# Two more batches of a fused attention and Fourier-mixing kernel take the folded token transform, under a new table of priorities

## The chip, the cores and the metric

The kernel runs on one NeuronCore of one Trainium2 chip. The metric is device time in microseconds (us). Before the change three runs gave 577.18, 578.38 and 578.51 us; their median is 578.38. One further execution, the profiled one, took 576.98 us, and every duration quoted below is from it. Its instructions span 575.2 us; the remaining 1.8 us lie around them.

The names of the engines in the profile: PE is TensorE (matrix products), PEld its weight loads, DVE is VectorE, ACT is ScalarE, POOL is GpSimd, and SP issues transfers.

## The reference

For 8 batches, 12 heads, 448 tokens and head size 64, the kernel computes cosine attention, a real-valued Fourier mix over tokens and features, a normalisation and a two-layer network:

```python
q_n = q / (norm(q) + 1e-6);  k_n = k / (norm(k) + 1e-6)
attn = softmax(q_n @ k_n.T / tau)            # per head
x = (attn @ v), heads side by side           # (8, 448, 768)
X = fft(x, axis=tokens); X = fft(X, axis=features)
u = x + real(X)
un = (u - mean(u)) / sqrt(var(u) + 1e-6)
out = u + relu(un @ w_ch1) @ w_ch2           # 768 -> 3072 -> 768
```

## The kernel before

**Planner.** The program does not write its instruction order by hand. Each step is an `Op` with a name such as `qk00_4` (step, then batch), a duration from a table (`TIMES`), a priority and its dependencies. `Plan.schedule` (line 257) plays the program through in modelled time and takes, on every engine, the ready step with the lowest priority number among those that can start first. The result is a fixed order of instructions for each of the queues PE, ACT, DVE, POOL and SP, with semaphores between them. After all steps are made, line 729 adds a number from the table `SHIFT` to the priority of single steps by name and occurrence. So `SHIFT` moves steps within the order, and nothing else. A step that may run on ACT or DVE goes where the planner finds room.

**Work of one batch.** (1) `norm` or `first_norm`: load q and k, square them on ACT (line 883), sum them on DVE (885), scale them (on POOL from batch 2 on, line 896), transpose them. (2) `attn`: for each of 6 pairs of heads the scores `qk` on PE (line 973 for three key tiles, two heads each on half of the rows; line 986 for the tail of 64 keys), the exponential on ACT (951), the products with v on PE (1004, 1010), the division on DVE (1028, 1030). (3) `fold`: sums and differences of mirrored tokens (n and 448-n) and of mirrored features on DVE (1047, 1054, 1081, 1098). (4) `fsum`: the transform over tokens on PE (1138 or 1134), evacuated by ACT or DVE (1159, 1160). (5) `fft`: the transform over features on PE (1188, 1191), its halves joined on DVE (1222) and added to x, with the sum for the mean (1233). (6) normalisation on ACT and DVE (1270 to 1282), a transpose by DMA, and (7) `ffn`: the two-layer network on PE (1350, 1445, 1494), with its evacuations (1366, 1514, 1530) and sums (1593).

**Interleaving.** Products of the network have a priority number above 5000, so that they fill PE wherever the attention and transform of the next batch have nothing ready. The network of batch b therefore lies between the pieces of attention and transform of batch b+1.

**The token fold.** `TF` (line 26) is 4, and a batch b with b >= TF handles its tokens differently. The 449 query columns of a score product (225 for tokens 0 to 224, 224 and one more for the mirrored ones) are given in four slices of 128, 97, 128 and 97 columns instead of two of 225 (`parts`, lines 936 to 938), so that token n and token 224-n meet at the same partition. Then `fold` multiplies half of its result by a mask (`z`, line 1091), forms sums and differences of tokens n and 224-n (`hb`, line 1094), and `fsum` needs for every frequency one product where it had two to add up (line 1134 instead of 1138; 16 products of 113 columns in a batch instead of 16 of 225). The table of cosines for this is rewritten once, in place, after the last unfolded batch (`ct`, line 1146). Because token 224 stands elsewhere, `fft` adds one more row (line 1258, one partition of 768 elements), and the lists of row numbers for the scattered output are made separately (`IDX2`, lines 626 to 632). How the scores of a batch are grouped into steps does not depend on `TF`: batches 1 to 3 take two key tiles in a step, batches 4 to 7 take three (lines 958 to 963).

Of the kernel before, what the change touches and what calls it, by code (L numbers as in the profile page):

```python
# [25 lines left out]
TF = 4  # L26
# [54 lines left out]
    "iotad": {0: 76.7149}, "tpd": {1: 15.2941}, "ktd0": {0: 169.0303}, "ix3": {0: -59.6164}, "ix4": {0: 735.3976}, "vz1": {0: 116.8365},  # L81
    "pads": {0: 761.6515}, "sins": {0: 15.0098}, "ldt0": {0: 217.8585}, "ldt1": {0: -95.8889}, "sind": {0: -207.551}, "sinp": {0: 240.8715},
# [1715 lines left out]
```

## Time and profile before

| | |
|---|---|
| profiled execution | 576.98 us |
| its span | 575.2 us, 16313 instructions |
| PE busy | 555.8 us, 97% of the span |
| DVE busy | 430.6 us, 75% |
| ACT busy | 385.3 us, 67% |
| POOL busy | 220.3 us, 38% |
| DMA | 62.20 MB, mean 108 GB/s |

A share of the span is a mean over very different stages. A table by stage (the view of windows) says in which stage an engine is full, the view of waits says for whom PE waited, and the chain that ended last gives single steps in order of time with the time each of them took before the next one began.

### The profile page before, as it was taken

How to read it: one execution, taken by the hardware profiler on the slowest of the kernel's cores; microseconds unless marked ns; L12 is line 12 of the kernel's file. 1: busy time of each engine (PE TensorE's matmuls, PEld its weight loads, DVE VectorE, ACT ScalarE, POOL GpSimd, SP SyncE). 2: the span in 40 equal slices, each digit the busy share in tenths (PEclk: the TensorE clock that was granted, in tenths of full speed). 3: DMA queues.
4: the chain of work that ended last, by engine and by line, in shares of the span. 5: the costliest groups of instructions: out<-in, count | busy, mean ns of one | idle time of the engine just before them, and what ended most of it. 6: DMA issues, size and time to landing. Idle time of an engine off the chain costs nothing.

```text
span 575.2 us, 16313 instructions
## 1 busy us (share of the span) xinstructions
PE 555.8 (97%) x6766; PEld 436.2 (76%) x6766; DVE 430.6 (75%) x917; ACT 385.3 (67%) x724; POOL 220.3 (38%) x332
## 2 busy tenths in 40 slices
PE   3899999999999999999999999999999999989997
PEld 3569787676787686878788787778778787959694
DVE  8989968996669869975669669776778579986262
ACT  7898885564876885687558875577637853747270
POOL 7534414356329544612370724523270210041303
PEclk9999999999999999999999999999999999999999
DMA  9999999975459739952595429743591210023001
GB/s 188 224 233 171 166 186 130 171 152 111 111 94 103 178 76 135 142 127 62 112 121 93 102 80 147 150 84 85 89 113 29 43 57 28 2 43 72 28 28 56
DMA packets 187898, 62.20 MB, mean 108 GB/s; under 512 B 166800, under 2 KB 185616, under 8 KB 187824
## 3 DMA queue, kind: packets, MB, share of 16 engines
q1 hardware_dynamic: 129856, 38.35, 33.7%
q0 software_dynamic: 57968, 22.81, 30.9%
q8 instruction: 53, 0.87, 0.6%
q14 instruction: 21, 0.17, 0.1%
HBM read 51.90 MB, written 11.01 MB: 109 GB/s over the span
## 4 chain that ended last, share of the span: by engine, by line
PE 60%; DVE 4%; ACT 2%; issue 0%; DVEq 0%; ACTq 0%
PE PS L1494 23%; PE PS L1350 20%; PE PS L1445 6%; PE PS L1010 4%; PE PS L973 3%; DVE U L1233 1%; PE PS L1004 1%; PE PS L986 1%; ACT E L951 1%; DVE ACG L1222 1%; ACT F L1275 1%; PE PS L1134 1%; PE PS L1191 1%; DVE SM L885 1%; DVE HQ L1593 1%
## 5 line engine op out<-in xcount | busy, mean ns | idle before, releaser
L1350 PE MATMUL PS<-UNT,W1b 128*128 128x256 bf16 (+1 forms) x1872 | 186.1, 256 | 1.2 <-DMA UNT<-F 0.6
L1350 PEld LDWEIGHTS PS<-UNT,W1b 128*128 128x128 bf16 x1872 | 155.5, 98 | 20.1 <-issue 2.7
L951 ACT ACTIVATE E<-PS 128x900 bf16<-128x900 f32 (+1 forms) x192 | 148.0, 827 | 19.1 <-PE PS L973 16.6
L1494 PE MATMUL PS<-W2b,HQ 128*128 128x384 bf16 x768 | 133.1, 326 | 0.0
L896 POOL TENSOR_TENSOR QH<-STG,SM 128x256 bf16<-128x256 f32 x126 | 82.3, 679 | 91.9 <-DVE SM L702 73.3
L1494 PEld LDWEIGHTS PS<-W2b,HQ 128*128 128x128 bf16 x768 | 73.3, 98 | 46.2 <-issue 0.7
L1519 POOL TENSOR_TENSOR OUTB<-OUTB,U 128x192 f32<-128x192 f32 x66 | 43.2, 675 | 138.5 <-ACT OUTB L1514 137.3
L1366 ACT ACTIVATE HQ<-PS 128x512 bf16<-128x512 f32 x81 | 48.2, 595 | 40.0 <-PE PS L1350 39.5
L1494 PE MATMUL PS<-TX,HQ 128*128 128x384 bf16 (+2 forms) x408 | 69.7, 321 | 1.8 <-ACT MV L1278 1.6
L883 ACT ACTIVATE QH<-STG 128x384 f32<-128x384 f32 x84 | 42.7, 520 | 25.8 <-DVE SM L885 21.3
L1494 PEld LDWEIGHTS PS<-TX,HQ 128*128 128x128 bf16 x408 | 38.4, 98 | 25.7 <-ACT MV L1278 2.0
L1593 DVE TENSOR_TENSOR HQ<-HQ 128x1536 bf16<-128x1536 bf16 (+1 forms) x69 | 49.5, 721 | 9.9 <-ACT HQ L1366 7.1
L885 DVE TENSOR_REDUCE SM<-QH 128x6 f32<-128x384 f32 x84 | 44.7, 544 | 11.3 <-ACT QH L883 11.0
L1010 PE MATMUL PS<-VB,E 128*128 128x65 bf16 x1152 | 51.4, 193 | 0.0
L1366 DVE TENSOR_SCALAR HQ<-PS 128x512 bf16<-128x512 f32 x45 | 31.0, 688 | 23.8 <-PE PS L1350 23.4
L1010 PEld LDWEIGHTS PS<-VB,E 128*128 128x128 bf16 x1152 | 47.7, 97 | 1.2
L1552 POOL DMA_INDIRECT out_dram<-OUTB,IDX x21 | 23.8, 1134 | 56.9 <-DVE OUTB L1530 51.7
L1004 PE MATMUL PS<-VZ,E 128*128 128x130 bf16 x192 | 41.6, 219 | 0.5 <-ACT E L951 0.2
L973 PE MATMUL PS<-QK 64*128 64x225 bf16 (+2 forms) x864 | 39.6, 227 | 0.1
L1233 DVE SCALAR_TENSOR_TENSOR U<-ACG,X 128x768 bf16<-128x768 f32 (+4 forms) x39 | 39.1, 1015 | 0.8
L1530 DVE TENSOR_TENSOR OUTB<-PS,OUTB 128x384 f32<-128x384 f32 x33 | 18.2, 553 | 25.7 <-PE PS L1494 21.9
L1514 ACT ACTIVATE OUTB<-PS 128x384 f32<-128x384 f32 x33 | 16.1, 488 | 29.5 <-PE PS L1494 29.1
(191 smaller groups left out, 793.6 us busy)
## 6 DMA issues: line engine op xcount, KB each, us to landing
STG<-in_q_dram SPq DMA_DIRECT2D x18, 384.0 KB, 4.0
STG<-in_k_dram SPq DMA_DIRECT2D x18, 384.0 KB, 3.8
VB<-in_v_dram POOLq DMA_DIRECT2D x24, 192.0 KB, 7.1
W1b<-in_moe_w_ch_dram POOLq DMA_DIRECT2D x12, 384.0 KB, 7.7
W2b<-in_moe_w_ch_dram POOLq DMA_DIRECT2D x12, 384.0 KB, 7.2
out_dram<-OUTB SPq DMA_DIRECT2D x7, 384.0 KB, 3.4
W2b<-in_q_dram SPq DMA_DIRECT2D x2, 576.0 KB, 10.0
W2b<-in_k_dram SPq DMA_DIRECT2D x2, 576.0 KB, 10.7
```

What stands on the lines that cost most here:

```text
L885: P.add("dve", lambda v, o=SS[:, i, H // ns * x:H // ns * (x + 1)], sq=sq: v.tensor_reduce(o, sq.rearrange("p (h d) -> p h d", d=DH), AX.X ...
L896: r = v.tensor_tensor(v3(qh)[:, h:h + 4], v3(buf)[:, h:h + 4], RN[:, i, h:h + 4].unsqueeze(2).to_broadcast((128, 4, DH)), AluOp.mult)
L951: return a.activation(o, self.PS[:, bk:bk + nc_, 0:SQ2], ACTF.Exp, scale=1.0 / self.tau)
L973: i = pe.matmul(self.PS[:, bk + h, c0:c0 + n], self.KT[r, jj, kt * 128:(kt + 1) * 128], self.QT[r, jj, cols], start=True, stop=True)
L1004: r = pe.matmul(o, st(6), self.VZ[:, j, :], start=not split, stop=(split and i == 0), skip_group_check=True)
L1010: r = pe.matmul(o[:, 65 * h:65 * h + 65], st(2 * kt + h), self.VB[:, kt, 2 * j + h, :], start=(split and i == h == kt == 0), stop=((not sp ...
L1233: self.snu.append(P.add("dve", lambda v: v.scalar_tensor_tensor(two(U[o0:o0 + n, ut, :]), src, 1.0, two(X[i0:i0 + n, x, :]), AluOp.mult, A ...
L1350: r = pe.matmul(self.PS[:, bk, x * n:(x + 1) * n], self.W1b[:, j, ft * 128:(ft + 1) * 128], self.UNT[:, j, cs], start=(j == 0), stop=(j == ...
L1366: return e.activation(o, i, ACTF.Relu) if e is self.nc.scalar else e.tensor_relu(o, i)
L1494: r = pe.matmul(self.PS[:, bk, 0:n], lhs(f), rhs(f), start=(start and f == 0), stop=(stop and f == NF // 2 - 1), skip_group_check=True)
L1519: r = g.tensor_tensor(self.OUTB[:, ob, xs], self.OUTB[:, ob, xs], self.U[:, ut, xs], AluOp.add)
L1593: P.add("dve", lambda v: v.tensor_tensor(cs(o), cs(a), cs(bq), op), 0.16 + 0.3 * len(ks), -0.5, f"{nm}{ks[0]}_{b}", reads=rd, writes=[x fo ...
```

## The change

`TF` becomes 2, and `SHIFT` is replaced as a whole. With `TF = 2` batches 2 and 3 use the fold as well. Everything that hangs on `b >= TF` follows: the four slices of the scores, the mask and the sums and differences of tokens, the shorter transform over tokens, the extra row, the rewriting of the cosine table after batch 1 instead of batch 3 (its priority is `100 * TF - 30`), and the row numbers of batches 2 and 3 in `IDX2` (made at priority `100 * TF + 50`). The old `SHIFT` names 312 steps and the new one 259; 111 names stand in both, and none of them has the same numbers in both.

```diff
-TF = 4
+TF = 2
 ORDER = (0, 1, 2, 3, 5, 4)
...
 SHIFT = {
-    "iotad": {0: 76.7149}, "tpd": {1: 15.2941}, "ktd0": {0: 169.0303}, "ix3": {0: -59.6164}, "ix4": {0: 735.3976}, "vz1": {0: 116.8365},
...
-    "s20_6": {0: -63.875}, "s40_6": {0: 409.5401}, "pq1_7": {0: -731.42, 1: -731.4499}, "ba1_7": {0: -695.7517}, "un3_7": {0: -225.5474}
+    "cst": {0: 20.1137}, "iotad": {0: 21.0782}, "ktd0": {0: 208.375}, "ix4": {0: 236.3035}, "vz1": {0: 43.4606}, "pads": {0: 210.9237},
...
+    "g1_7": {0: -224.2779, 1: -228.6318}, "S12": {0: -9.2904}, "c31_6": {1: 538.5408}, "fin10_6": {0: 556.2734}, "s40_6": {0: 583.647},
+    "fin21_6": {0: 581.6738}, "u0_7": {0: -147.96, 1: -244.7591}, "pq1_7": {0: -244.8056, 1: -534.8029}, "u1_7": {0: -246.0651, 1: -217.4615},
+    "u224_7": {0: -205.1433}, "ba0_7": {0: -246.1099}, "un0_7": {0: -230.3877}, "ba1_7": {0: -224.4681}, "ba3_7": {0: -248.8728},
+    "un3_7": {0: -175.3393}
 }
```

More of the change, by code (lines that the diff above doesn't have):

```diff
@@ L80 @@
 SHIFT = {
-    "iotad": {0: 76.7149}, "tpd": {1: 15.2941}, "ktd0": {0: 169.0303}, "ix3": {0: -59.6164}, "ix4": {0: 735.3976}, "vz1": {0: 116.8365},
-    "pads": {0: 761.6515}, "sins": {0: 15.0098}, "ldt0": {0: 217.8585}, "ldt1": {0: -95.8889}, "sind": {0: -207.551}, "sinp": {0: 240.8715},
[59 rows of a table removed]
+    "cst": {0: 20.1137}, "iotad": {0: 21.0782}, "ktd0": {0: 208.375}, "ix4": {0: 236.3035}, "vz1": {0: 43.4606}, "pads": {0: 210.9237},
+    "sins": {0: -0.2698}, "sinp": {0: 176.095}, "half": {0: 83.4718}, "ldt": {0: 73.0886}, "ld_t0_0": {0: -9.2696}, "sqQ0_0": {0: -15.0619},
[49 rows of a table added]
 }
```

103 rows, old and new, of the table SHIFT are left out of this document.

## The prediction

> **What bounds the kernel now.** I read the table by stage first, with the stages cut where the batches change, then the waits of PE after 60 us, then the chain that ended last. Columns of the table: stretch, its length, busy us (and instructions) of PE, weight loads, DVE, ACT and POOL, granted clock, DMA share, GB/s.
>
> ```profile
> span 575.2 us, 16313 instructions
> PE 555.8 (97%) x6766; PEld 436.2 (76%) x6766; DVE 430.6 (75%) x917; ACT 385.3 (67%) x724; POOL 220.3 (38%) x332
> ```
> ```profile
> 0.00:14.00 14.00, 4.77 (x51) 4.25 (x52) 12.21 (x27) 10.20 (x19) 11.28 (x39) 1.00 1.14 189
> 14.00:60.00 46.00, 42.38 (x649) 33.76 (x647) 42.23 (x110) 41.57 (x77) 21.77 (x27) 1.00 1.33 203
> 60.00:575.00 515.00, 508.65 (x6070) 398.21 (x6070) 376.13 (x782) 333.50 (x631) 187.29 (x268) 1.00 0.58 98
> 75.00:103.00 28.00, 28.00 (x330) 21.78 (x328) 20.08 (x45) 19.27 (x34) 10.37 (x15) 1.00 1.13 158
> 182.00:236.00 54.00, 53.84 (x571) 39.40 (x568) 44.27 (x97) 39.30 (x81) 28.38 (x40) 1.00 0.74 117
> 236.00:301.00 65.00, 64.91 (x842) 51.98 (x841) 45.34 (x96) 43.18 (x82) 27.17 (x39) 1.00 0.65 118
> 571.00:575.20 4.20, 0.70 (x13) 0.53 (x10) 0.71 (x2) 0.00 (x0) 0.97 (x1) 0.90 0.26 94
> ```
> ```profile
> PE PS L1494 <- ACT MV L1278: 1.6, 1, 1.6
> PE PS L1350 <- DMA UNT<-F: 0.6, 1, 0.6
> PE PS L1350 <- DVE QK L799: 0.3, 1, 0.3
> PE PS L986 <- ACT E L951: 0.2, 1, 0.2
> ```
>
> From 60 us on PE is busy for 508.65 of 515 us. Of the 6.35 us left, 3.5 are the last store (4.20 - 0.70) and 2.7 are the four waits listed (1.6 + 0.6 + 0.3 + 0.2). The clock is granted in full. So from 60 us on the order hides nearly everything behind PE, and a microsecond of PE work less is a microsecond of time less, as long as the order stays as good. Ahead of 60 us it is another matter: DVE is busy 42.23 of 46 us, ACT 41.57, and PE misses 9.2 us before 14 us (14.00 - 4.77) and 3.6 after it (46.00 - 42.38). There the order on DVE and ACT decides, and what is lost there stays lost.
>
> **PE work, part by part.** The case is comfortable, since batches 4 to 7 already do what batches 2 and 3 will do. The chain gives the steps of both kinds; columns: start us, time on the chain, engine, output, line, number of instructions.
>
> ```profile
> 199.61 0.49 PE PS L973 x8
> 204.17 1.42 PE PS L1350 x12
> 213.01 1.31 PE PS L1350 x12
> 231.74 1.58 PE PS L1138 x16
> 261.30 0.71 PE PS L973 x24
> 297.54 0.83 PE PS L1134 x16
> 320.70 1.95 PE PS L1494 x12
> ```
>
> Transform over tokens: 16 products take 1.58 us unfolded and 0.83 us folded. That is 0.75 us less in each batch, 1.50 us in two.
>
> Scores: an unfolded step of two key tiles has 8 products and takes 0.49 us; a folded step of three tiles has 24 and takes 0.71. Batches 2 and 3 keep steps of two tiles, now with 16 products, a size that the trace doesn't have. From below, in proportion to the folded row, it is 0.71 x 16/24 = 0.47 us. From above, it is the unfolded row and 8 products more at their fixed cost. This fixed cost follows from two rows: 12 products of 256 columns take 1.31 us (0.109 each) and 12 of 384 take 1.95 (0.1625), so a column costs 0.42 ns and about 2 ns a product are fixed; 0.49 + 8 x 0.002 is 0.51. I take 0.50, nearer the upper end, because its row is the same step on the same two tiles. With 9 such steps in a batch (72 products of 8 a step) this costs 9 x 0.01 = 0.1 us a batch, 0.2 us in two, and -0.4 to +0.4 between the ends. The tail of the scores costs nothing more, with 2 or with 4 products:
>
> ```profile
> 146.15 0.37 PE L986 MATMUL PS<-QK,KTD 128*128 128x225 bf16 x2
> 146.36 0.81 PE L1494 MATMUL PS<-W2b,HQ 128*128 128x384 bf16 x4
> 258.32 0.36 PE L986 MATMUL PS<-QK,KTD 128*128 128x128 bf16 x4
> 258.52 2.78 PE L1350 MATMUL PS<-UNT,W1b 128*128 128x256 bf16 x24
> ```
>
> From its start to the next product's start it is 0.21 us with two and 0.20 with four. The other products of the batch are unchanged in number and shape, so the PE work falls by 1.50 - 0.20 = 1.30 us (1.1 to 1.9).
>
> The folded row of 0.83 us for 16 products is 52 ns a product. Against it stands a rule of the Trainium skill, "TensorE: Matmul & The Clock Gate", section "Back-to-back issue gap": in a stream of weight loads and products a product of 128 columns sustains about 81 ns, since the load counts too. By that page's figure 16 short products would be 1.30 us (an estimate from it) and the fold would save 0.28 us a batch, not 0.75. The trace disagrees by its 52 ns, so the measurement goes into the sum.
>
> **DVE, ACT and POOL work.** Groups by line, with form, count, busy us and mean ns:
>
> ```profile
> L1094 DVE TENSOR_TENSOR F<-ACG 128x772 bf16<-128x772 bf16 x8 | 4.2, 558 | 0.0
> L1233 DVE SCALAR_TENSOR_TENSOR U<-ACG,X 1x768 bf16<-1x768 f32 x4 | 4.0, 1011 | 0.1
> L1091 ACT ACTIVATE ACG<-ACG,MV 128x772 bf16<-128x772 bf16 x4 | 3.8, 939 | 2.7 <-DVE ACG L1081 2.7
> ```
>
> A folded batch adds two sums of 0.56 us and one row of 1.01 us on DVE, 2.1 us, and a mask of 0.94 us on ACT (less if it falls to DVE). Batch 3's stretch (182 to 236) has 54.00 - 44.27 = 9.7 us of DVE and 14.7 us of ACT to spare. I cost these at nothing. Their cover is PE's filling with network products; without it they are latency, and this can be measured on the chain from the last division of attention to the first transform product:
>
> ```profile
> 226.06 0.69 DVE L1030 TENSOR_TENSOR X<-PS,RD 128x512 bf16<-128x512 f32 x1
> 289.34 0.69 DVE L1030 TENSOR_TENSOR X<-PS,RD 128x512 bf16<-128x512 f32 x1
> ```
>
> Unfolded it is 231.74 - 226.75 = 5.0 us, folded 297.54 - 290.03 = 7.5 us. With 0.75 us less in the transform and the row of 1.0 us behind it, a folded batch reaches its normalisation 2.5 - 0.75 + 1.0 = 2.75 us later. The stretch of batch 4 (236 to 301), which contains this longer chain, has PE idle for 0.09 us of 65. So the cover holds where it could be seen.
>
> The four copies of the cosine table (one on DVE, three on ACT; 0.2 to 0.3 us each by the two rows below) move from batch 3 to batch 1, where the stretch 75 to 103 has 8 us of DVE free and PE loses nothing. They are queued on DVE and ACT ahead of the next batch's work; the folded transform of batch 2 waits for them, and that comes tens of microseconds later. The row numbers for batches 2 to 7 are small steps on POOL, moved ahead by 200 in priority and past the scaling of q and k there; POOL has 17.6 us to spare in 75 to 103. Both cost nothing in the sum, and at most about 1 us each if they came in front of a step that PE waits for.
>
> ```profile
> L1686 ACT ACTIVATE CS<-CS x3: 284/285/312, 235.0 to 235.6; 128x98 bf16<-128x98 bf16 x1, 128x128 bf16<-128x128 bf16 x1, 128x96 bf16<-128x96 bf16 x1
> L1687 DVE COPY CS<-CS x1: 165/165/165, 234.8 to 234.8; 128x128 bf16<-128x128 bf16 x1
> ```
>
> **The new order.** This is the part without a row of its own: every queue, SP's and POOL's too, may change its order. Bounds: at best it takes away the four waits after 60 us (-2.7) and the 3.6 us that PE misses between 14 and 60 us, -6.3 in all; at worst it adds as much as it could take away, since nothing in the rows says which way a step goes. One of these waits can be looked at:
>
> ```profile
> 503.48 1.28 DVE L1593 TENSOR_TENSOR HQ<-HQ 128x1536 bf16<-128x1536 bf16 x1
> 504.68 0.14 DVE L1270 TENSOR_SCALAR MV<-ACG 128x1 f32<-128x1 f32 x1
> 505.22 0.96 DVE L1593 TENSOR_TENSOR HQ<-HQ 128x1536 bf16<-128x1536 bf16 x1 [0.39 <-DVE MV L1270]
> 506.32 0.97 PE L1494 MATMUL PS<-TX,HQ 128*128 128x384 bf16 x5 [1.64 <-ACT MV L1278]
> ```
>
> PE starts again at 506.32, right after DVE's second long sum (505.22 + 0.96), though the view names ACT. That sum stood behind the adds of batch 7's rows. The new table gives new numbers to many steps just there (`u1_7`, `u224_7`, `ba1_7`, `fin10_6`), so this wait will hardly come out the same; I take half of it, -0.8 us. For the opening I take 0, the middle of its bounds.
>
> **Sum.** -1.3 (PE work) - 0.8 (half a wait) = -2.1 us. The profiled execution of 576.98 becomes 574.9. The median of the runs, 578.38, lies 1.4 us above the profiled one; taken to the median the forecast is 578.38 - 2.1 = 576.3 us, 0.36% faster. A measurement of this kernel can tell about 0.3% (1.7 us) from no change, so the forecast lies barely outside.
>
> **Rivals.** *The opening gets worse (slower).* Place: DVE and ACT between 14 and 60 us, 92% and 90% busy, where the new table moves the tables' and constants' steps and the first scalings (`cst`, `sinp`, `half`, `scQ0_0`, `scK1_0`, `ek1_0`). PE has no slack later, so a wait there stays. For: that stretch is the fullest, and depends on when loads land. Against: the same steps are done, none is added. Price: if PE's missing 3.6 us double, +3.6 - 1.3 = +2.3, 580.7 us. It decides from 1.3 us of new waiting on, and beyond 0.3% from 3.0.
>
> *The longer chain isn't covered (slower).* Place: between the fold and the normalisation of batches 2 and 3. Price: 2 x 2.75 - 1.3 = +4.2, 582.6 us, if nothing covers it. Against: the 0.09 us of batch 4. It decides from 1.3 of 5.5 us uncovered.
>
> *The saving is eaten by small waits (no change).* The PE work falls as said, but the new order brings 1 to 2 us of waits elsewhere: 578 us. For: waits of 0.2 to 1.6 us exist in the old order too.
>
> *The new order is better throughout.* All four waits go and the opening gains 1 us: -1.3 - 2.7 - 1.0 = -5.0, 573.4 us.
>
> **How the numbers follow.** Chances: forecast 0.45 (own range 574.5 to 577.5), better throughout 0.12, no change 0.13, opening worse 0.22, chain uncovered 0.08. Of the forecast's 0.45 a fourth lies within 0.3%. So faster is 0.12 + 0.34 = 0.46; within 0.3% is 0.11 + 0.10 = 0.21, the rest of the no-change case going to slower; slower is 0.30 + 0.03 = 0.33. The range for 8 in 10 goes from 573.0, just under the best case, to 581.0, just over the opening's price; outside stay most of the chain case and the tails of both ends.
>
> **What would show it.** In the changed profile the 225-column products of line 973 should number 144 instead of 288, line 1134's 113-column products 96 instead of 64, and line 1138's fall by 32; PE's steps in batches 2 and 3 should take 0.83 us for the transform and 0.47 to 0.51 for a score step of 16. The stretch from 60 us on should show PE idle by less than 3 us before the last store. The prediction is wrong if PE's idle time ahead of 60 us differs by more than 1.5 us from 12.8 (9.2 + 3.6), if a wait of over 1 us for DVE or ACT stands in batches 1 to 3, or if the step of 16 takes more than 0.55 us.

## The result, and the profile after

The changed kernel takes 583.08 us (median of six runs, 581.28 to 584.71) against 578.33 us for the kernel before on the same chip (577.18 to 578.51). The ratio is 1.0082 with a 95% interval of 1.0060 to 1.0103: the change makes the kernel slower by 0.8%, where the forecast was 576.3 us. The profiled execution took 582.74 us; its span is 5.6 us longer than that of before.

Lines of the changed kernel stand 10 lower than those of before (line 1350 became 1340). First the head of its page:

```profile
span 580.8 us, 16703 instructions
...
PE 558.0 (96%) x6952; PEld 439.1 (76%) x6952; DVE 431.2 (74%) x923; ACT 385.3 (66%) x728; POOL 218.9 (38%) x332
```

The first three rows of the table by stage, with the columns of the prediction (stretch, length, busy us and instructions of PE, weight loads, DVE, ACT and POOL, granted clock, DMA share, GB/s):

```profile
0.00:14.00 14.00, 4.44 (x36) 3.50 (x36) 11.94 (x29) 9.53 (x17) 11.15 (x38) 1.00 1.00 181
14.00:60.00 46.00, 42.07 (x627) 33.87 (x627) 40.95 (x102) 40.44 (x72) 19.65 (x25) 0.96 1.32 198
60.00:580.80 520.80, 511.49 (x6291) 401.73 (x6289) 378.33 (x794) 335.31 (x642) 188.13 (x271) 1.00 0.60 97
```

PE's eight largest waits from 60 us on (what PE waited for: us in total, times, the longest):

```profile
PE PS L1484 <- DVE OUTB L1520: 1.1, 2, 0.8
PE PS L994 <- ACT E L941: 0.9, 1, 0.9
PE PS L1124 <- DVE F L1088: 0.7, 1, 0.7
PE PS L1340 <- DVE KTD L833: 0.7, 1, 0.7
PE PS L1340 <- DMA UNT<-F: 0.6, 1, 0.6
PE PS L1435 <- DMA UNT<-F: 0.6, 1, 0.6
PE PS L963 <- DMA QK<-QH: 0.4, 1, 0.4
PE PS L1340 <- DVE OUTB L1520: 0.4, 1, 0.4
```

The 5.6 us can be put together from PE's side. Ahead of 60 us PE is idle for 13.5 us (9.56 + 3.93) instead of 12.8, which is 0.6 more. From 60 us on it is idle for 9.3 us (520.80 - 511.49) instead of 6.55 (515.2 us after the cut at 60, less 508.65), which is 2.8 more: the four waits of before made 2.7 us, the eight listed here make 5.4. And PE is busy 2.2 us longer (558.0 against 555.8), although its useful work fell. That is the last thing to explain, and the groups by line and form show it, of the kernel after and then of the kernel before (count | busy us, mean ns | idle time before them):

```profile
L1727 PE MATMUL PS<-TX 128*128 128x128 bf16 x150 | 13.9, 247 | 8.7 <-DVE U L605 7.5 <-DVE RD L1018 0.5 <-DVE HQ L655 0.2
L963 PE MATMUL PS<-QK 64*128 64x225 bf16 x144 | 11.5, 271 | 0.4 <-DVE RD L1018 0.2
L1727 PE MATMUL PS<-W1b 128*128 128x128 bf16 x24 | 1.7, 220 | 0.2 <-DVE U L1223 0.2
```
```profile
L973 PE MATMUL PS<-QK 64*128 64x225 bf16 x288 | 21.0, 259 | 0.1
L1737 PE MATMUL PS<-TX 128*128 128x128 bf16 x150 | 12.8, 236 | 8.7 <-DVE SM L762 7.6 <-DVE SM L701 0.6 <-DVE SM L702 0.3
L1737 PE MATMUL PS<-W1b 128*128 128x128 bf16 x6 | 0.5, 219 | 0.0
```

Line 1727 (1737 before) holds products that compute nothing; the program puts them into holes of the order. There are 18 more of them on W1b, 1.2 us. The 24 of the changed kernel stand at 511.7 to 513.6 us, and the next useful product (513.59) starts as DVE's evacuation of a result (line 1520, at 512.98 for 0.55 us) is done, so this is waiting in another form. The 150 others are as many as before but take 1.1 us more. The 144 score products of 225 columns take 11.5 us; the same ones of batches 0 and 1 took 10.8 us before (21.0 less the 10.2 us of batches 2 and 3), so 0.7 more. Both fit a stretch at half clock in the opening, shown below. 1.2 + 1.1 + 0.7 less the 1.1 us of saved work, worked out next, is 1.9 of the 2.2 us. The half clock is not why the kernel is slower: four of its six runs had the clock granted in full, and they took 581.3 to 583.6 us.

### The profile page after: what moved, and what is told of

It is laid out like the page before. It is cut to its first block, busy times and chain, and to the rows that moved or that the text cites. A ratio compares the mean times of both kernels' runs of the same rounds, so it can differ in the third digit from the quotient of the medians.

```text
span 580.8 us, 16703 instructions
## 1 busy us (share of the span) xinstructions
PE 558.0 (96%) x6952; PEld 439.1 (76%) x6952; DVE 431.2 (74%) x923; ACT 385.3 (66%) x728; POOL 218.9 (38%) x332
## 4 chain that ended last, share of the span: by engine, by line
PE 72%; DVE 13%; DMA 5%; POOL 4%; ACT 3%; issue 2%; SPq 0%; POOLq 0%; DVEq 0%; ACTq 0%
PE PS L1340 26%; PE PS L1484 24%; PE PS L1435 7%; PE PS L963 5%; PE PS L1000 4%; DMA W1b<-in_moe_w_ch_dram 2%; DMA QK<-QH 2%; DVE HQ L1583 2%; PE PS L994 1%; PE PS L976 1%; ACT E L941 1%; DVE U L1223 1%; DMA UNT<-F 1%; DVE X L1020 1%; DVE ACG L1212 1%
## 5 line engine op out<-in xcount | busy, mean ns | idle before, releaser
L1509 POOL TENSOR_TENSOR OUTB<-OUTB,U 128x192 f32<-128x192 f32 x66 | 41.3, 646 | 131.3 <-ACT OUTB L1504 131.1
L1356 ACT ACTIVATE HQ<-PS 128x512 bf16<-128x512 f32 x90 | 53.6, 596 | 44.3 <-PE PS L1340 43.6
L1484 PEld LDWEIGHTS PS<-TX,HQ 128*128 128x128 bf16 x408 | 37.9, 98 | 25.7 <-DVE OUTB L1520 2.4
L1542 POOL DMA_INDIRECT out_dram<-OUTB,IDX x21 | 22.8, 1084 | 75.9 <-DVE OUTB L1520 33.8
L873 ACT ACTIVATE QH<-STG 128x384 f32<-128x384 f32 x84 | 42.9, 520 | 10.2 <-DVE SM L875 7.5
L963 PE MATMUL PS<-QK 64*128 64x128 bf16 (+1 forms) x1008 | 40.5, 220 | 0.8 <-DMA QK<-QH 0.4
L1356 DVE TENSOR_SCALAR HQ<-PS 128x512 bf16<-128x512 f32 x36 | 24.8, 689 | 19.8 <-PE PS L1340 19.5
L963 PEld LDWEIGHTS PS<-QK 64*128 64x128 bf16 x1008 | 27.6, 95 | 13.7 <-issue 6.5
```

The costliest lines, as they stand in the source:

```text
L873: P.add("act", lambda a, sq=sq, src=buf[:, w * x:w * x + w]: a.activation(sq, src, ACTF.Square), t_act(w), pr, f"sq{i}_{b}", reads=bn, wri ...
L963: i = pe.matmul(self.PS[:, bk + h, c0:c0 + n], self.KT[r, jj, kt * 128:(kt + 1) * 128], self.QT[r, jj, cols], start=True, stop=True)
L1356: return e.activation(o, i, ACTF.Relu) if e is self.nc.scalar else e.tensor_relu(o, i)
L1484: r = pe.matmul(self.PS[:, bk, 0:n], lhs(f), rhs(f), start=(start and f == 0), stop=(stop and f == NF // 2 - 1), skip_group_check=True)
```

## The forecast's PE work, step by step

Steps of batch 3 in the changed kernel, in order of time (start us, duration, engine, line, products, idle time before); the time of a step is from its start to the next row's start:

```profile
189.88 0.58 PE L963 MATMUL PS<-QK 64*128 64x128 bf16 x16
190.39 2.77 PE L1484 MATMUL PS<-W2b,HQ 128*128 128x384 bf16 x16
```
```profile
235.40 0.99 PE L1124 MATMUL PS<-CS,F 128*128 128x113 bf16 x16
236.23 0.81 PE L1484 MATMUL PS<-W2b,HQ 128*128 128x384 bf16 x4
```

The folded score step of 16 products takes 0.51 us, the folded transform 0.83 us. Both are as forecast. Over two batches that is -1.50 us and 18 times 0.02 us, so about -1.1 us of PE work. This part of the change does what it says. The rest of the loss lies in waits, some of them filled with products that compute nothing, and the question for the experiments is whose they are: the fold's or the new order's.

## The experiments

In the experiments' kernels the order of every queue is written out as a list (step names, with # and the occurrence), taken from what the planner made of the kernel before (old order) or after (new order), and then edited; the planner only gives times and semaphores to it. Their lines stand about 131 higher than in the kernel before. Ratios are to the kernel before on the same chip, with 95% intervals. The planner still puts its filler products into every hole that its planned times show, so their number differs between these kernels. They count as busy, so a list of PE's waits misses the time that they cover. On W1b there are 6 of them in the kernel before, `old_open_new`, `old_moved`, `old_tuned` and `fold_tuned`; 24 in the changed kernel, `new_open_old` and `early_new`; 36 in `new_no_fold`; 42 in `norm_first`, `mended` and `fold3_on_old`; 66 in `fold_on_old` and `fold_no_dve`; 84 in `late_new`. No run leaves them out.

Theories at the start: A, the loss arises in the new opening; B, it arises later in the new order; C, it is the fold's longer chain, uncovered; D, the fold is free where the order is good.

**Fold alone, and order alone.** `fold_on_old` is the old order with the fold in batches 2 and 3, each added step right behind what it needs; `new_no_fold` is the new order without the fold.

```diff
 # fold_on_old: old order
-TF = 4
+TF = 2
```

> The fold in batches 2 and 3 with all queues in the order of the kernel before; the eight added steps (mask, two sums and one row for each batch) and the four copies of the cosine table stand right behind the last step that they need. Theory C (the longer chain is not covered unless the order is made for it): the PE work falls by 1.3 us, but PE waits up to 2.75 us in each of the two batches, 578.3 - 1.3 + 5.5 = 582.5 us, with waits of over 1 us ahead of the transform of batches 2 and 3. Theory D (PE's filling covers it without any new order): 578.3 - 1.3 = 577.0 us.

```diff
 # new_no_fold: new order
-TF = 2
+TF = 4
```

> The order of the changed kernel without the fold in batches 2 and 3 (the eight steps are dropped, the copies of the cosine table go back behind batch 3). If the order alone is what costs time: the changed kernel's 583.1 plus 1.3 us of PE work, 584.4 us. If the fold's longer chain is what costs time in batches 2 and 3: the waits ahead of the transform of batch 2 (0.90 and 0.45 us), and of the scores' exponentials behind it (1.04 us), are gone, 584.4 - 2.4 = 582.0 us.

Measured: `fold_on_old` 584.00 us, ratio 1.0085 (1.0068 to 1.0101); `new_no_fold` 584.54 us, ratio 1.0079 (1.0054 to 1.0103). Each alone costs as much as both together (1.0082), so the two costs don't add. On the new order the fold makes no difference that can be told: its 1.1 us of saved PE work lie within the intervals. The chain into batch 2's network shows a place where the two overlap. It runs from the last division of batch 2's attention on DVE (start plus 0.69) to the first product of its network on PE. Before, after, `new_no_fold` and `fold_on_old`, in this order:

```profile
172.74 0.69 DVE L1030 TENSOR_TENSOR X<-PS,RD 128x512 bf16<-128x512 f32 x1
...
194.85 4.76 PE L1350 MATMUL PS<-UNT,W1b 128*128 128x256 bf16 x42
```
```profile
174.67 0.69 DVE L1020 TENSOR_TENSOR X<-PS,RD 128x512 bf16<-128x512 f32 x1
...
200.93 3.34 PE L1340 MATMUL PS<-UNT,W1b 128*128 128x256 bf16 x29
```
```profile
174.70 0.69 DVE L1161 TENSOR_TENSOR X<-PS,RD 128x512 bf16<-128x512 f32 x1
...
201.11 2.79 PE L1481 MATMUL PS<-UNT,W1b 128*128 128x256 bf16 x24
```
```profile
173.90 0.69 DVE L1162 TENSOR_TENSOR X<-PS,RD 128x512 bf16<-128x512 f32 x1
...
198.27 2.79 PE L1482 MATMUL PS<-UNT,W1b 128*128 128x256 bf16 x24 [0.48 <-DMA UNT<-F]
```

The chain takes 21.4 us before (194.85 - 173.43). On the old order the fold makes it 23.7 us, 2.3 us longer, near the 2.75 that the prediction priced for an uncovered chain. In the new order it takes 25.6 us with the fold and 25.7 without. So the new order stretches this chain by 4.3 us with no fold in it, and the fold's longer path disappears in that.

On the old order C also shows in PE's own rows, under filler products (line 1869 of `fold_on_old`) right ahead of the folded transforms (line 1266) of batches 2 and 3:

```profile
179.01 1.51 PE L1869 MATMUL PS<-W1b 128*128 128x128 bf16 x24 [0.16 <-DVE F L1226]
180.48 1.03 PE L1266 MATMUL PS<-CS,F 128*97 128x113 bf16 x16
...
236.31 1.14 PE L1869 MATMUL PS<-W1b 128*128 128x128 bf16 x12
237.57 1.00 PE L1266 MATMUL PS<-CS,F 128*128 128x113 bf16 x16
```

Both transforms start 0.06 us after the end of DVE's last step for them (line 1230, at 180.42 and 237.51). So 1.5 and 1.3 us here are waits for the fold, at the two places that C named. DVE is not simply full there: in both batches it waits itself, 1.14 and 1.08 us, for ACT's mask (line 1223) before it can form the sums. The length of the chain counts as well as the room on DVE.

Where time is lost can be followed along the network's 1152 products of 384 columns that read HQ, each set against the one with the same number in the kernel before. `fold_on_old` lags by 1.2 us at 177 us, 6.4 at 251 and 7.5 at 294, and by no more than 7.8 after that. The changed kernel lags by 2.5, 5.5 and 3.3 at the same places, then by 3.3 at 466 and 6.3 at 540; `new_no_fold` by 2.5, 7.1, 5.1, 5.7 and 8.6. So on the old order the fold loses in batches 2 and 3, and what is lost there stays. The new order loses in the opening, in batches 2 and 3 even without the fold, and again behind 466 us. D falls on the old order and C holds there; the cost of the new order by itself is A or B, which the next pair separates.

**The opening.** `old_open_new` has the new order up to the first product of batch 0's network (about 50 us) and the old one behind it; `new_open_old` is the reverse, with the fold.

```diff
 # old_open_new: old order, no fold
-up to h0_0: old order
+up to h0_0: new order
```

> The reverse: no change to the kernel before but the opening (all that is planned ahead of the first network product of batch 0), which stands in the order of the changed kernel. Theory A: 578.3 + 2.4 = 580.7 us, the first network product ends near 51.4 us instead of 49.0. Theory B: 578.3 within 0.5 us.

```diff
 # new_open_old: new order, fold
-up to h0_0: new order
+up to h0_0: old order
```

> The changed kernel (fold in batches 2 and 3) with all queues in the changed kernel's order, except that everything planned ahead of the first network product of batch 0 stands in the order of the kernel before. Theory A (the opening's order costs time that never comes back): the first network product ends 2.4 us earlier than in the changed kernel (49.0 instead of 51.4 us), and the whole is 2.4 us shorter, 580.7 us. Theory B (the opening's lag is hidden later by PE's filling, and the loss is all in batches 2 and 3): within 0.5 us of the changed kernel's 583.1.

Measured: `old_open_new` 579.97 us, ratio 1.0020 (1.0006 to 1.0035), so the new opening costs about 1.1 us by itself. `new_open_old` 583.53 us, ratio 1.0068 (1.0050 to 1.0086): taking the new opening back gains nothing that can be told from the changed kernel. The forecast's rival "the opening gets worse" is real but small; it is not the larger part of the 4.7 us. Whether its 1.1 us come through in the changed kernel stays open, since the two intervals are as wide as that.

**Batch 3 alone.** `fold3_on_old` folds from batch 3 on. Batches 2 and 3 share a tile that is laid out for both folded or both not, so their values are not right here; the amount of work is that of one more folded batch.

```diff
 # old order
-TF = 4
+TF = 3
```

> The fold in batch 3 only (batch 2 unfolded), all queues in the order of the kernel before, the four added steps and the copies of the cosine table right behind what they need. With the fold in both batches on that order the kernel lagged by about 9 us at equal PE work behind batch 3, of which some 4.5 us for each batch if they cost alike: 578.9 + 4.5 - 0.65 = 582.7 us. If batch 2 is the costly one, where the network products of batch 1 run out just when those of batch 2 become ready, batch 3 alone costs 2 us at most: below 580.9 us.

Measured: 582.45 us, ratio 1.0070 (1.0053 to 1.0087). One folded batch costs nearly what two cost (1.0085, on another chip), so the price isn't simply per batch, and batch 2 is not the one that carries it.

**The fold without its DVE and ACT work.** `fold_no_dve` is `fold_on_old` with the mask, the sums and the differences of tokens cut to 2 of 193 columns in batches 2 and 3, and their added row dropped. So the folded tokens of these batches are not computed, and PE's work stays.

```diff
-                z = gp(G[:], [[4 * NG, 2], [2 * NG, 2], [1, NG]], NG)
+                nz = 2 if b < 4 else NG
+                z = gp(G[:], [[4 * NG, 2], [2 * NG, 2], [1, nz]], NG)
...
-                if b >= TF:
+                if b >= 4:
```

> The fold in batches 2 and 3 on the order of the kernel before, with the DVE and ACT work that it adds left out: the mask and the two sums run over 2 columns of 193 instead of all, and the added row is dropped in these two batches, so the transform there works on incomplete data. PE does all of the folded work. Theory C (the added DVE and ACT work sits on the path to the network's first product and costs more than PE saves): most of the 5.2 us by which the full fold on this order is slower than the kernel before goes, to 579.5 us or less; with the three steps' fixed times left, not below 577.6 (all of PE's 1.3 us saved). Theory G (it is not their work but the other columns, evacuations and copies of the fold): 583 to 584 us.

Measured: 580.84 us, ratio 1.0048 (1.0032 to 1.0065). Against `fold_on_old` some 0.37% or 2.1 us go with the added DVE and ACT work, so this work was not free. Its share is larger than that. The planner's table of durations still has the full steps, so the 60 filler products that it added in `fold_on_old` stay, and now they stand where PE need not wait:

```profile
179.83 1.50 PE L1870 MATMUL PS<-W1b 128*128 128x128 bf16 x24
...
234.82 0.83 PE L1870 MATMUL PS<-W1b 128*128 128x128 bf16 x12
```

DVE's last steps for the two transforms (line 1231) end at 180.11 and 234.52 us, and the transforms start at 181.17 and 235.49, behind the fillers. So about 1.1 + 0.7 us of the remaining 2.8 us (0.48%) are the fillers', an estimate from these rows. Followed along the network's products, this kernel loses 1.2 us between 177 and 294 us, where `fold_on_old` loses 6.3. In both kernels the copies of the cosine table stand ahead of evacuations of batch 1, which is a flaw of this insertion and not of the changed kernel; 18 fillers cover about 1.0 us there (102.32 to 103.33 in `fold_on_old`).

**The norm of batch 2, moved up.** In the new order the factor `rs1_2` on ACT and the normalisation `un1_2` on DVE stand behind work that they don't need. `norm_first` moves them.

```diff
-act: bs1_2 ex0_3#3 ln21_2 ex0_3#2 rs1_2
+act: bs1_2 ln21_2 rs1_2 ex0_3#3 ex0_3#2
-dve: u1_2#2 u1_2#3 u1_2#1 un1_2
+dve: u1_2#2 un1_2 u1_2#3 u1_2#1
```

> The changed kernel in its own order, but for three steps of batch 2's normalisation: on ACT the logarithm and the exponential of the second tile (ln21_2, rs1_2) come right behind its square instead of behind two exponentials of batch 3's scores, and on DVE the scaling of that tile (un1_2) comes behind the first of the three row additions instead of behind all. Theory E (the chain to the network's first product of batch 2 sets the time, since by then the network products of batch 1 are used up): the first product of batch 2 starts 1.5 to 2 us earlier than in the changed kernel, and the whole is 1.5 us shorter, 581.5 us. Theory F (the place in the queue doesn't matter, PE has other work): 583.1 within 0.5 us.

Measured: 583.30 us, ratio 1.0102 (1.0080 to 1.0124). The theory of this run falls. `un1_2` did end 1.7 us earlier, but PE's queue is in order, and in it the network's first product stands behind value products of batch 3 that wait for ACT's exponentials. In `norm_first` 18 more filler products stand there too, and the network's first product starts at 201.42 us, in the changed kernel at 200.93. The changed kernel's trace has the wait:

```profile
199.35 0.23 PE L994 MATMUL PS<-VZ,E 128*128 128x130 bf16 x1 [0.87 <-ACT E L941]
```

**Three mends together.** `mended` is the changed kernel with `norm_first`'s edit, with the network's first product `h0_2` ahead of that value product, and with two steps of the opening put back.

```diff
-act: sqK1_0 sqQ2_0 et0_0#1 eq0_0 ek0_0
+act: sqK1_0 et0_0#1 eq0_0 ek0_0 sqQ2_0
-pool: W1_7 W1_8 sinp
+pool: W1_7 sinp W1_8
-pe: pv10_3 pv11_3 qk20_3 h0_2
+pe: h0_2 pv10_3 pv11_3 qk20_3
```

> The changed kernel with three places of its order put as before has them or better: on ACT the square of the late load (batch 0, group 2) behind the three evacuations that it held up; on POOL the negated sine table ahead of one weight load; in batch 2 the norm's factor on ACT and the normalisation on DVE right behind what they need, and on PE the first network product of batch 2 ahead of the value product that waits for the exponentials. If each wait of PE counts in full: 1.0 + 0.7 + 1.0 us less, about 580.5 us. If the waits form again at the next place, since DVE and ACT are full there (as with the whole opening of before, which gained nothing): 582.5 to 583.5 us.

Measured: 588.82 us, ratio 1.0178 (1.0156 to 1.0200), so three mends made it slower still. In its profiled execution (585.87 us, the fastest of five) the wait for the transposes of batch 7's normalised rows, 0.6 us in the changed kernel, is now the largest:

```profile
524.70 1.51 PE L1576 MATMUL PS<-UNT,W1b 128*128 128x128 bf16 x24 [2.41 <-DMA UNT<-F]
```

**Half old, half new.** `early_new` is the changed kernel up to the first network product of batch 3 (`h0_3`, about 260 us) and the old order from there on; `late_new` is the old order up to there and the new one behind it, without the fold.

```diff
 # early_new (fold)
-from h0_3 on: new order
+from h0_3 on: old order
```

> The changed kernel up to the first network product of batch 3 (about 260 us), fold in batches 2 and 3 included, and the order of before from there to the end. If the loss arises in the stretch up to 260 us, as the ledger of PE's waits says (4 us of opening and waits in batches 2 and 3, less the 1.2 us of PE work that the fold saves), this is about 582.5 us. If the early waits are taken up again later and the late part of the new order is what costs, about 579.5 us.

```diff
 # late_new (no fold)
-from h0_3 on: old order
+from h0_3 on: new order
```

> The counterpart: before, no fold in batches 2 and 3, with the order of before up to the first network product of batch 3 and the changed kernel's order from there on. If the loss arises up to 260 us: about 579 us (the late part of the new order has waits of 0.3 to 0.8 us at five places, 2.4 us in all, in place of the 1.8 us at 504 us). If the late part costs: 581 to 582 us.

Measured: `early_new` 587.01 us, ratio 1.0144 (1.0115 to 1.0173); `late_new` 584.63 us, ratio 1.0110 (1.0088 to 1.0131). Neither expectation holds. `early_new` loses more than the whole new order; `late_new` loses about as much as `new_no_fold` (1.0079) or more, since the intervals overlap. At least in `late_new` much of it arises at the joint: 54 filler products, 3.9 us, stand between 255 and 264 us. So this pair doesn't tell which half costs; these two orders cannot be cut in the middle and judged by halves.

**The old order's own waits.** If waits are the loss, the old order should gain where its two largest are taken away. `old_moved` does that, without the fold.

```diff
-dve: c31_6#3 u1_7 s12_6 u224_7 s30_6 ba0_7 s20_6 u1_7#1 fin10_6
+dve: c31_6#3 s12_6 s30_6 s20_6 u1_7 fin10_6 u224_7 ba0_7 u1_7#1
-act: fa1_6#2 bs0_7 ln20_7 rs0_7 bs1_7 fv1_6 ln21_7 rs1_7 fm1_6
+act: fa1_6#2 fv1_6 bs0_7 ln20_7 rs0_7 bs1_7 fm1_6 ln21_7 rs1_7
...
-act: sq4_2#0 sq4_2#1 bs1_1 ln21_1 rs1_1
+act: sq4_2#0 bs1_1 ln21_1 rs1_1 sq4_2#1
-dve: u1_1#1 ss4_2#0 ba1_1 un0_1 u1_1#2 ss4_2#1 ba3_1 ba2_1 fin20_0 un1_1
+dve: u1_1#1 ba1_1 ss4_2#0 un0_1 u1_1#2 un1_1 ss4_2#1 ba3_1 ba2_1 fin20_0
```

> Before, no fold in batches 2 and 3, with only the two largest waits of its PE taken on. At 504 us: on DVE the sums that the network's products of batch 6 wait for go ahead of batch 7's row adds (and the evacuation that frees the bank right behind), on ACT that step's two copies ahead of batch 7's biases. At 117 us: batch 1's second normalisation ahead of two squares' sums of batch 2. If both waits (1.8 and 0.8 us) lie on the path and nothing else is late: about 575.8 us. If what was moved back is late next: 577.5 to 578.5 us.

Measured: 578.63 us, ratio 1.0006 (0.9993 to 1.0020), no change. So writing an order out as a list costs nothing by itself. The waits of its PE in batch 1 and around 505 us, with the wait of before in batch 1 below them (its 1.64 us at 506.32 stands in the prediction):

```profile
119.10 6.72 PE L1482 MATMUL PS<-UNT,W1b 128*128 128x256 bf16 x60 [0.38 <-DVE OUTB L1662]
126.17 1.05 PE L1482 MATMUL PS<-UNT,W1b 128*128 128x256 bf16 x8 [0.35 <-ACT HQ L1498]
...
505.68 4.06 PE L1626 MATMUL PS<-TX,HQ 128*128 128x384 bf16 x24 [0.47 <-DVE HQ L1725]
...
514.32 1.96 PE L1626 MATMUL PS<-TX,HQ 128*128 128x384 bf16 x11 [0.68 <-DVE OUTB L1662]
```
```profile
117.90 9.33 PE L1350 MATMUL PS<-UNT,W1b 128*128 128x256 bf16 x84 [0.62 <-DMA UNT<-F]
```

In batch 1 one wait of 0.62 us became two of 0.38 and 0.35. Around 505 us one of 1.64 became 0.47 and 0.68; what is left of the gain is lost again before the end. The edits did what they should at their place, and the next evacuations (lines 1662 and 1498) were late in turn.

**The last two: can the fold be placed better, and does any new order cost?** `fold_tuned` puts the fold's steps into the old order by a search of small moves between 95 and 270 us; `old_tuned` is the control, the same search without the fold over the whole span. The search judged orders by the program's own planned times. The changed kernel, for comparison, has 231 of PE's 969 steps and 280 of DVE's 818 common steps out of the old sequence.

```diff
 # fold_tuned: fold in 2 and 3; steps moved against fold_on_old
+pe 19 of 969, act 78 of 696, dve 92 of 864, pool 18 of 195
 # old_tuned: no fold; steps moved against before
+pe 32 of 969, act 174 of 693, dve 270 of 859, pool 51 of 195
```

> Fold in batches 2 and 3 as in the changed kernel, on the order of before, with the added steps put in by a search of small moves between 95 and 270 us (19 of 969 steps of PE, 78 of 696 of ACT, 92 of 864 of DVE stand elsewhere than in the plain insertion). If the fold costs by itself, since DVE has no room for its 2 us per batch where they fall, it stays slower than before: 581 to 582.5 us, of the 584.0 that the plain insertion took. If only the places of the steps were bad, PE's 1.2 us of saved work show: 577 to 578.5 us.

> The control: before, no fold in batches 2 and 3, with its order changed by the same kind of search over the whole span (32 steps of PE, 174 of ACT, 270 of DVE, 51 of POOL moved; as many on DVE as the changed kernel moves). If a new order costs only where it brings the waits that the changed kernel shows (batches 2 and 3, the opening), this one is no slower than before: 577 to 579 us. If so many moves cost by themselves, whatever they were for: 581 us or more, like the changed kernel's order without the fold (584.5 us).

Measured: `fold_tuned` 583.06 us, ratio 1.0073 (1.0057 to 1.0090); `old_tuned` 588.06 us, ratio 1.0157 (1.0140 to 1.0174). The control shows that a large reordering with nothing added can cost 1.6%, twice what the change costs. It is one order, chosen by planned times; on DVE it moves about as many steps as the changed kernel, on PE far fewer. Its first network product of batch 0 starts at 51.35 us instead of 48.46, so 2.9 us of its loss lie in the opening. And the fold, placed by a search on the old order, is as slow as in the new one. In that kernel PE waits most for DVE's sums of the network (line 1725, three times):

```profile
PE PS L1626 <- DVE HQ L1725: 3.7, 3, 1.6
```

The first of the three stands right behind the folded transform of batch 2, on its own trace:

```profile
184.03 0.82 PE L1626 MATMUL PS<-TX,HQ 128*128 128x384 bf16 x4 [1.60 <-DVE HQ L1725]
```

## Why the prediction was wrong, by its steps

**PE work: right.** -1.30 us was forecast, about -1.1 us came (0.51 us for the score step, against 0.50 taken; 0.83 for the transform). The 225-column products at line 963 number 144, and line 1124's 113-column products 96, as said.

**What the prediction would take as a sign of being wrong hardly showed.** PE was idle for 13.5 us ahead of 60 us (within 1.5 of 12.8), no wait in batches 1 to 3 was over 1 us, and the step of 16 took 0.51. Only one expectation failed: from 60 us to the end of its last product (575.91 + 2.14 us) PE was idle for 6.6 us (9.3 less the 2.75 behind it), not for less than 3.

**"I cost these at nothing": wrong.** This is the first step that failed. The cover was argued from 9.7 us of DVE slack in the stretch 182 to 236 and from the 0.09 us of batch 4, a mean over 54 us and another batch. The stretch does not even hold batch 2's fold, whose attention ends at 173.43 in the kernel before. Where the added steps fall there is no such slack. The changed kernel from 174 to 198 us, columns as above:

```profile
174.00:198.00 24.00, 22.98 (x242) 15.89 (x238) 22.96 (x51) 16.49 (x35) 14.68 (x18) 1.00 0.97 107
```

DVE is busy for 22.96 of 24 us, 96%. The kernel before is as full in its own stretch of batch 2, so a narrower window would have shown it:

```profile
172.00:196.00 24.00, 23.84 (x217) 16.62 (x215) 22.98 (x53) 16.75 (x37) 18.18 (x20) 1.00 1.12 133
```

DVE's steps around the fold in the changed kernel, and PE's:

```profile
179.14 1.41 DVE L1583 TENSOR_TENSOR HQ<-HQ 128x512 bf16<-128x512 bf16 x2
180.47 0.19 DVE L691 TENSOR_SCALAR SM<-SM 128x24 f32<-128x24 f32 x1
180.55 1.38 DVE L1084 TENSOR_TENSOR F<-ACG 128x772 bf16<-128x772 bf16 x2
181.85 0.29 DVE L692 RECIPROCAL SM<-SM 128x24 f32<-128x24 f32 x1
182.06 0.77 DVE L1088 TENSOR_TENSOR F<-F 128x388 bf16<-128x388 bf16 x2
182.75 1.36 DVE L1583 TENSOR_TENSOR HQ<-HQ 128x1536 bf16<-128x1536 bf16 x1
```
```profile
182.88 1.00 PE L1124 MATMUL PS<-CS,F 128*128 128x113 bf16 x16 [0.74 <-DVE F L1088]
184.17 2.12 PE L1484 MATMUL PS<-TX,HQ 128*128 128x384 bf16 x12 [0.28 <-DVE HQ L1583]
```

The fold's sums (line 1084) delay DVE's sum for the network (line 1583), and the other way round; PE waits for the one, then for the other, 1.0 us, about what the fold saves in PE work. On the old order the fold costs 0.85%, some 5 us, and at least 2.1 of them go with its DVE and ACT work. Rival "the longer chain isn't covered" (582.6 us, chance 0.08) described this on the old order; it was given too little.

**"-0.8, half of the wait at 504": wrong in what it left out.** The wait is gone from the list, but its place is not closed, and the step didn't say what is late next. In the changed kernel the 24 products that fill holes stand there now, 1.7 us (`L1727` on W1b, above), and behind them the 0.6 us for batch 7's transposes (`L1435`, in the list of waits). These 1.7 us and 0.6 us are more than the 1.64 us that went. `old_moved` shows the same on the old order: with the wait cut by its edit the time did not move.

**"For the opening I take 0": off by about 1.1 us**, as `old_open_new` has it; `new_open_old` can't tell how much of that remains in the changed kernel.

**The term "new order", bounds -6.3 to +6.3: mis-sized, and the largest part of the error.** -0.8 us was taken; the order without the fold measures +0.79%, 4.6 us. These are 5.4 of the 6.8 us between the forecast (-2.1) and the result (+4.7); the other 1.4, roughly, are the saving of 1.3 us that does not show. Each of these parts is uncertain by more than 1 us. The bounds held the term, but the middle was no sensible choice: the forecast took it that a step moved goes up or down alike. The new order itself, `old_tuned`, `mended` and the joined orders came out slower by 0.8 to 1.8% (`mended` and `early_new` have the fold too), the old order with the new opening by 0.2%, and `old_moved`, with about thirteen steps moved, came out equal. These are few orders, but none gained: on this kernel a new order is not a draw around zero. The hint stood in the prediction and was not used: where PE is idle for only 2.7 us in waits after 60 us, little can be gained and much lost.

What stays open: why the old order is so much better than others for the same work. That waits form anew at the next place is shown in `old_moved`; which property of the old order avoids it is not. The split of the changed kernel's loss between fold and order has no single answer either, since the two don't add. How much the filler products themselves cost, beyond the waits that they cover, is measured in no run.

## What to carry to other kernels

A step's cover has to be looked up where the step falls: beside a mean slack of 18% over 54 us (182 to 236) stood a stretch of 24 us with 4% (172 to 196). Where PE runs almost without a gap, taking a wait away can bring it back at the next step that was late behind it, as in `old_moved`; so a wait seen in the profile need not be the gain. A busy engine may be busy with fillers, so count them beside the waits. A change of work that comes with a new order should be measured in both parts, and beside a control that reorders about as much and adds nothing.

## What the runs showed of the hardware

*Half clock in the middle of the opening.* In the changed kernel's profile PE waits for 1.57 us and then runs with a mean granted clock of 0.72 from 14 to 20 us, where the kernel before has 1.00:

```profile
14.21 0.34 PE L798 MATMUL PS<-TX,QH 128*128 128x128 bf16 x3 [1.57 <-ACT KTD L833]
```
```profile
14.00:20.00 6.00, 5.71 (x64) 4.71 (x64) 4.85 (x10) 5.94 (x11) 2.85 (x6) 0.72 1.72 175
```

A loss of 0.28 over 6 us is 3.4 us at half clock. None of the other profiles here has it in this stretch. The Trainium skill, "TensorE: Matmul & The Clock Gate", section "What's actually happening", gives a free-running window of about 3.4 us after which an idle PE falls to half clock. The length agrees; the wait here was shorter than such a window, but PE was little busy ahead of it (4.44 of the first 14 us).

*DVE beside POOL.* The fold's two sums took 1.38 us at 180.55, where the forecast had 2 x 0.56. The second of them took 906 ns; the other eleven of line 1084 took 547 to 567. POOL ran two additions on the output tile at the same time:

```profile
180.81 1.53 POOL L1509 TENSOR_TENSOR OUTB<-OUTB,U 128x192 f32<-128x192 f32 x2 [0.19 <-ACT OUTB L1504]
```

The Trainium skill, "SBUF — State Buffer", section "SBUF: two separate sides", says that a DVE operation with two inputs in SBUF and a GpSimd operation that reads SBUF take one shared pair of ports in turn. The longer time agrees with that, and in `norm_first`, `new_open_old` and `fold_tuned` the one sum that ran beside two of POOL's additions took 907 to 910 ns. But no run here takes POOL's additions away.
